# A convolution and an MLP in one kernel: three store pairs go to GpSimd's queue, and two transform visits move half a step

## The chip, the cores and the metric

The kernel runs on one core of a Trainium2 chip. A core has five engines, each with an instruction queue of its own that it works through in order: TensorE (PE, matmuls, with its weight loads shown apart as PEld), VectorE (DVE), ScalarE (ACT), GpSimd (POOL) and SyncE (SP), which here only issues transfers. Transfers are issued from the queues of SP, ACT and POOL; an issuing instruction that must wait holds up all that stands behind it in the same queue. The metric is the device time of one execution in microseconds (us); the median of 3 runs of the kernel before is 369.38 us (369.35 to 369.51).

## The reference

The inputs are q, k and v (2048 x 448 each), and weights. All is float32.

```python
xn = layernorm(q)
# A: an H3 layer
k_shift = sum_t k[s - 3 + t] * shift_k[:, 3 - t]        # 4 taps, causal
kv = k_shift * v
y  = causal_conv(kv, ssm_k) + kv * ssm_D                # length 2048 per channel, by FFT
A  = xn * y
# B: an MLP
B  = mish(xn @ w1 + b1) @ w2                            # 448 -> 1792 -> 448
out = q + A + B
```

## The kernel before

**Two jobs share the engines.** The MLP is the backbone. Its 2048 rows are cut into 8 chunks of 256, its 1792 hidden columns into 7 pairs of two 128-column blocks; chunk and pair together are numbered 0 to 55, and this text calls one such number a pair. Every float32 operand of the matmuls is split into a high part (`XH`, `w1h`, `w2h`, `ach`; cast on ACT) and a low part (`XL`, `w1l`, `w2l`, `acl`; the subtraction on DVE), and three products are summed. The long convolution runs as a two-stage Fourier transform in matmuls of their own, of which only the first stage matters here.

**The order is written out by hand.** The main loop (L637) runs over half steps `s`. Pair i has its first-layer matmuls, g1 (`g1_mm`, L457, 22 matmuls into a psum tile `pg`), in half step 2i. In half step 2i + 1 ACT applies mish (`mish`, L465) to it and splits the result into `ach` (L74) and `acl` (L75). Its second-layer matmuls, g2 (`g2_mm`, L482 to L484), follow two pairs later: half step 2i + 1 holds g2 of pair i - 2. All else is hung onto half steps: `at(slot, ...)` puts a call in front of a half step's own work, `after(slot, ...)` behind it. Within each engine the instructions stand exactly in the order in which the code issues them.

**The weights stream in during chunk 0.** Pieces of w1 and w2 are loaded by SP through four buffers `kr`, split (`w1_split`: ACT L340, DVE L345 and L347; `w2_split`: ACT and DVE in `split`, L74 and L75) and so free the buffer for a later load. g1 of pair 2 in half step 4 needs w1's third piece, whose split is hung in front of half step 4; g2 of pair 2 in half step 9 needs w2's third piece, split after half step 7.

**The first transform stage.** h (the convolution's kernel, `hT`) and kv come in 8 groups each. One group takes a *visit*: `f1_mm` (L125, 8 matmuls into two psum tiles `pc`; there are two such tiles in all), then `f1_fold` (ACT copies one half into a buffer `st`, L131; DVE forms sum and difference, L132 and L134), then `f1_out` (L140), which stores `st` to the scratch tensor `Dh` in DRAM in two transfers, one for each half of the partitions. There are two `st` buffers, so the copy L131 of a group waits until the stores of the group two visits earlier have landed. The head group, group 1, has its visit in half step 1 and its stores in half step 4. The other groups of h have theirs by the table `H_AT` (group: half step); the stores come three half steps after the visit. Group 2 comes next, then 3, then 0. The load of a group's input is issued five half steps ahead of its visit.

**POOL** normalises the rows of chunks 1 to 6 (`ln_parts`: L388, L392, L396), takes one of the four taps of kv per group (L155), and issues transfers only late in the program (`e_load` L284, and those of the last stage).

Of the kernel before, what the change touches and what calls it, by code (L numbers as in the profile page):

```python
# [22 lines left out]

G2_LAG = 2
H_HEAD = 1
H_AT = {2: 4, 3: 8, 0: 12, 4: 16, 5: 20, 6: 26, 7: 32}
KV_AT = (24, 29, 34, 39, 44, 50, 55, 60)
POOL_H = {20: (0, 2)}
H0_AT = 63
# [9 lines left out]
def tile_kernel(ctx: ExitStack, tc, q, k, v, sk, hT, sD, w1, b1, w2, c_f1, c_g, c_gi, c_i2, out):  # L39
    nc = tc.nc  # L40
# [15 lines left out]
    Dh = dp.tile([NO * 16, 32, D], F32, name="Dh")  # L56
# [32 lines left out]
    plan, plan2 = {}, {}  # L89

    def at(slot, fn, *args):
        plan.setdefault(int(slot), []).append((fn, args))

    def after(slot, fn, *args):
        plan2.setdefault(int(slot), []).append((fn, args))
# [38 lines left out]
        V.tensor_sub(st[:, 1], e, st[:, 1])  # L134
        dv()

    def f1_out(dst, g, key):
        st = ST.pop((key, g))
        for jj in range(2):
            nc.scalar.dma_start(dst.rearrange("(h p) n d -> p h n d", h=2)[:, :, 4 * g + 2 * jj:4 * g + 2 * jj + 2].rearrange("p h n d -> p h (n d)"),  # L140
                                st[64 * jj:64 * jj + 64].rearrange("p h b d -> p h (b d)"))

    def k_load(g):
# [385 lines left out]

    for g, t in H_AT.items():  # L530
        if g != 2:
            at(t - 5 if t > 7 else t - 3, h_load, g)
        if g == 0:
            after(t - 2, lambda: V.tensor_add(HT[0][0:1, 0], HT[0][0:1, 0], SD.pop()))
        at(t, f1_mm, HT, g, "h")
        if t in POOL_H:
            after(t, taps_pool, *POOL_H[t])
        after(t, f1_fold, g, "h")
        at(t + 3, f1_out, Dh, g, "h")

    at(12, lambda: nc.sync.dma_start(skb, sk.partition_broadcast(128)))
    for g in range(-2, 0):
# [1 line left out]
    for g, t in enumerate(KV_AT):  # L544
        d = t - (KV_AT[g - 1] if g else t - 6)
        at(t - d - (3 if g > 1 else 2), k_load, g)
        at(t - d - 1, v_load, g)
        for u in range(4):
            after(t - (2 if g else 1) - d + d * u / 4, taps, g, u)
        at(t, f1_mm, KV, g, "kv")  # L550
        if g + 1 < NO:
            after(t, taps_pool, g + 1, 2)
        after(t, f1_fold, g, "kv")
        at(t + 3, f1_out, Dkv, g, "kv")
# [9 lines left out]
    for o in range(NO):  # L564
        s, d = OCT_AT[0] + OCT_AT[1] * o, OCT_AT[1]
        h = s - 1 if o else H0_AT
# [66 lines left out]
    w1_lo(0, 128, 256)  # L633
    plan.setdefault(1, []).insert(0, (f1_mm, (HT, H_HEAD, "h")))
    plan2.setdefault(1, []).append((f1_fold, (H_HEAD, "h")))
    plan.setdefault(4, []).insert(0, (f1_out, (Dh, H_HEAD, "h")))
    for s in range(nslots):  # L637
        j = s // 2 - G2_LAG - 1
        if s % 2 == 0 and j >= 0 and pairs[j][1] == NP - 1:
# [75 lines left out]
```

## Time and profile before

| what | value |
|---|---|
| median of 3 runs | 369.38 us (369.35 to 369.51) |
| the profiled execution | 370.86 us |
| its span, first to last instruction | 368.9 us |
| granted TensorE clock over the span | 1.0 |
| PE busy | 98% |
| DVE, ACT, POOL busy | 71%, 45%, 19% |
| transfers, all queues | 79.35 MB, mean 215 GB/s |
| stores of h (`Dh<-st`), 16 of 448 KB, issued by ACT | 6.4 us to landing (median) |

A row of a timeline begins with the start in us from the span's beginning and the duration in us; then come engine, line, operation, output<-inputs, sizes, a count, and in brackets the idle time ahead of it with the work that ended it. Rows of groups end with the busy time in us, the mean of one in ns, and the idle time ahead. ACTq, SPq and POOLq are the parts of these engines that issue transfers. A wait row reads: who waited for whom, total us, times, longest.

### The profile page before, as it was taken

The numbers are of one execution on the slowest core, as the hardware profiler recorded it, in microseconds if no ns is written. First come the engines' busy times: TensorE is split into PE (matmuls) and PEld (weight loads), VectorE is DVE, ScalarE is ACT, GpSimd is POOL, SyncE is SP. The second block draws the span as 40 slices with busy tenths as digits, with TensorE's granted clock in tenths as the row PEclk, the third lists the DMA queues.
The fourth block names the chain that finished last, engine by engine and source line by source line (L and its number), as shares of the span: only waits on it lengthen the run. The fifth ranks groups of instructions, "written<-read, shape, count | busy, mean of one in ns | idle before, by whom it ended". The sixth has DMA issues, their size and how long they took to land.

```text
span 368.9 us, 7464 instructions
## 1 busy us (share of the span) xinstructions
PE 360.9 (98%) x3128; PEld 292.6 (79%) x3128; DVE 262.5 (71%) x359; ACT 166.3 (45%) x277; POOL 71.2 (19%) x58
## 2 busy tenths in 40 slices
PE   7998999999999999999999999999999999999995
PEld 2697888978888989889868666666666889889885
DVE  5897858999998888996515657656385752897751
ACT  3757543344241443253254555556655533235450
POOL 2005000920228222611006000060000005102020
PEclk9999999999999999999999999999999999999999
DMA  7998996839496329514675598896694375949655
GB/s 241 346 285 312 358 368 184 256 105 295 105 299 214 89 66 274 170 48 101 225 244 174 194 261 238 282 301 189 209 292 125 95 248 205 419 195 276 116 66 133
DMA packets 32354, 79.35 MB, mean 215 GB/s; under 512 B 2881, under 2 KB 19138, under 8 KB 32322
## 3 DMA queue, kind: packets, MB, share of 16 engines
q1 hardware_dynamic: 20210, 44.09, 35.8%
q10 hardware_dynamic: 9776, 22.88, 22.2%
q0 software_dynamic: 2336, 11.93, 11.3%
q8 instruction: 24, 0.39, 0.4%
q14 instruction: 8, 0.07, 0.1%
HBM read 50.44 MB, written 28.44 MB: 214 GB/s over the span
## 4 chain that ended last, share of the span: by engine, by line
PE 71%; DMA 12%; DVE 9%; POOL 3%; ACT 2%; issue 2%; SPq 0%; ACTq 0%; POOLq 0%; DVEq 0%
PE pg L457 27%; PE pg L482 10%; PE pg L484 9%; PE pg L483 9%; PE pc L208 7%; DMA kr<-in_w_dram 6%; PE pc L251 4%; PE pc L125 2%; PE pc L308 2%; DMA Dh<-st 2%; DVE x L172 2%; PE pg L407 2%; POOL xn L392 2%; DMA Dkv<-st 1%; DMA av<-Dkv 1%
## 5 line engine op out<-in xcount | busy, mean ns | idle before, releaser
L465 ACT ACTIVATE a<-pg,b1t 128x256 f32<-128x256 f32 x112 | 47.1, 472 | 113.0 <-PE pg L457 88.2
L457 PE MATMUL pg<-XH,w1h 128*128 128x256 f32 x448 | 91.3, 285 | 0.9 <-ACT XH L419 0.9
L75 DVE TENSOR_TENSOR acl<-a,ach 128x512 fp32r<-128x512 f32 x56 | 38.8, 693 | 65.0 <-ACT ach L74 64.7
L457 PEld LDWEIGHTS pg<-XH,w1h 128*128 128x128 f32 x448 | 69.6, 188 | 18.9 <-issue 15.7
L482 PE MATMUL pg<-w2h,ach 128*128 128x448 f32 x224 | 83.1, 371 | 0.0
L483 PE MATMUL pg<-w2l,ach 128*128 128x448 f32 x224 | 81.3, 363 | 0.9 <-DVE w2l L75 0.9
L484 PE MATMUL pg<-w2h,acl 128*128 128x448 f32 x224 | 81.4, 363 | 0.0
L457 PE MATMUL pg<-XL,w1h 128*128 128x256 f32 x448 | 69.6, 277 | 0.2 <-DVE XL L417 0.2
L457 PEld LDWEIGHTS pg<-XL,w1h 128*128 128x128 f32 x448 | 59.4, 188 | 0.4 <-DVE XL L417 0.4
L457 PE MATMUL pg<-XH,w1l 128*128 128x256 f32 x336 | 56.8, 277 | 0.0
L482 PEld LDWEIGHTS pg<-w2h,ach 128*128 128x128 f32 x224 | 42.0, 188 | 11.7 <-issue 9.4
L457 PEld LDWEIGHTS pg<-XH,w1l 128*128 128x128 f32 x336 | 46.8, 188 | 0.0
L483 PEld LDWEIGHTS pg<-w2l,ach 128*128 128x128 f32 x224 | 42.1, 188 | 3.6 <-DVE w2l L75 1.2
L484 PEld LDWEIGHTS pg<-w2h,acl 128*128 128x128 f32 x224 | 42.1, 188 | 2.5
L388 POOL TENSOR_TENSOR rstd<-ve,mhalf 128x2 f32<-128x2 f32 (+1 forms) x9 | 8.8, 977 | 156.2 <-DVE ve L385 156.1
L74 ACT CAST ach<-a 128x512 fp32r<-128x512 f32 x56 | 34.7, 620 | 1.8
L155 POOL TENSOR_TENSOR x<-kr,skb 128x896 f32<-128x896 f32 x8 | 17.1, 2133 | 83.6 <-DVE x L154 62.4
L392 POOL TENSOR_SCALAR xn<-qt,mv,rstd 128x448 f32<-128x448 f32 x12 | 27.8, 2320 | 0.6
L172 DVE TENSOR_TENSOR x<-x 128x896 f32<-128x896 f32 x24 | 26.8, 1115 | 1.4 <-POOL x L155 0.9
L131 ACT COPY st<-pc 128x896 f32<-128x896 f32 x16 | 14.5, 906 | 14.5 <-PE pc L125 12.6
L132 DVE TENSOR_TENSOR st<-pc,st 128x896 f32<-128x896 f32 x16 | 17.4, 1088 | 3.6 <-ACT st L131 3.1
L259 ACT COPY qe<-pc 128x896 f32<-128x896 f32 x16 | 13.8, 912 | 11.0 <-PE pc L251 10.8
(70 smaller groups left out, 389.7 us busy)
## 6 DMA issues: line engine op xcount, KB each, us to landing
Dh<-st ACTq DMA_DIRECT2D x16, 448.0 KB, 6.4
Dkv<-st ACTq DMA_DIRECT2D x16, 448.0 KB, 5.1
ah<-Dh SPq DMA_DIRECT2D x8, 896.0 KB, 7.0
av<-Dkv SPq DMA_DIRECT2D x8, 896.0 KB, 6.2
E<-qe ACTq DMA_DIRECT2D x16, 448.0 KB, 5.2
e<-E POOLq DMA_DIRECT2D x8, 896.0 KB, 7.9
kr<-in_k_dram SPq DMA_DIRECT2D x10, 448.0 KB, 6.7
x<-in_v_dram SPq DMA_DIRECT2D x8, 448.0 KB, 5.2
```

What stands on the lines that cost most here:

```text
L74: nc.scalar.copy(h, raw)
L75: V.tensor_sub(l, raw, h)
L132: V.tensor_add(st[:, 0], e, st[:, 1])
L155: nc.gpsimd.tensor_mul(o, KR[g - u // 2], skb[:, u:u + 1].to_broadcast([128, 2, D]))
L172: V.tensor_add(KV[g], KV[g], o)
L208: nc.tensor.matmul(p[32 * t:32 * t + 32, r, :D], g[rs, t, c], a[rs, t], start=True, stop=True, tile_position=(64 * r, 32 * t))
L392: eng.tensor_scalar(xn[:, jj, :D], Q[c][:, jj], mv[:, j, 0:1], rstd[:, j:j + 1], op0=ALU.subtract, op1=ALU.mult)
L457: nc.tensor.matmul(ps[:, n], l, r, start=n_ == 0, stop=n_ == len(mm) - 1)
L465: nc.scalar.activation(a[:, n], ps[:, n], AF.Mish, bias=b1t[:, 2 * p + n:2 * p + n + 1])
L482: nc.tensor.matmul(ps, ah[:, n, cs], w2h[:, f], start=f == 0, stop=False)
L483: nc.tensor.matmul(ps, ah[:, n, cs], w2l[:, f], start=False, stop=False)
L484: nc.tensor.matmul(ps, al[:, n, cs], w2h[:, f], start=False, stop=f == NF - 1)
```

## The change

`f1_out` gets the issuing engine as an argument. The head group's stores, and those of the groups whose visit stands before half step 12 (groups 2 and 3), are issued by GpSimd; those of the other five groups of h, and all of kv, stay with ScalarE. The visits of groups 2 and 3 move from half steps 4 and 8 to 5 and 9, and with them the fold, the stores (now in front of half steps 8 and 12) and group 3's load (from half step 3 to 4).

```diff
-H_AT = {2: 4, 3: 8, 0: 12, 4: 16, 5: 20, 6: 26, 7: 32}
+H_AT = {2: 5, 3: 9, 0: 12, 4: 16, 5: 20, 6: 26, 7: 32}
...
-    def f1_out(dst, g, key):
+    def f1_out(dst, g, key, eng=nc.scalar):
         st = ST.pop((key, g))
         for jj in range(2):
-            nc.scalar.dma_start(dst.rearrange("(h p) n d -> p h n d", h=2)[:, :, 4 * g + 2 * jj:4 * g + 2 * jj + 2].rearrange("p h n d -> p h (n d)"),
+            eng.dma_start(dst.rearrange("(h p) n d -> p h n d", h=2)[:, :, 4 * g + 2 * jj:4 * g + 2 * jj + 2].rearrange("p h n d -> p h (n d)"),
                                 st[64 * jj:64 * jj + 64].rearrange("p h b d -> p h (b d)"))
...
-        at(t + 3, f1_out, Dh, g, "h")
+        at(t + 3, f1_out, Dh, g, "h", nc.gpsimd if t < 12 else nc.scalar)
...
-    plan.setdefault(4, []).insert(0, (f1_out, (Dh, H_HEAD, "h")))
+    plan.setdefault(4, []).insert(0, (f1_out, (Dh, H_HEAD, "h", nc.gpsimd)))
```

The first place is PE at half step 4, with the waits of each instruction in brackets (the numbers name semaphores; `pg_216` is g1 of pair 1, `pg_269` before and `pg_259` after are g1 of pair 2). Before:

```order
L457 MATMUL pg_216<-XL,w1h 128x256 x4
L125 MATMUL pc<-x,f1id 64x448 [waits DMAHW1_49,Activation_49]
L125 MATMUL pc<-x,f1id 64x448
L125 MATMUL pc<-x,f1id 64x448 [waits DVE_49]
L125 MATMUL pc<-x,f1id 64x448 x5
L457 MATMUL pg_269<-XH,w1h 128x256 [waits Activation_49]
L457 MATMUL pg_269<-XH,w1h 128x256 x2
L457 MATMUL pg_269<-XH,w1l 128x256 [waits DVE_49]
```

After:

```order
L457 MATMUL pg_216<-XL,w1h 128x256 x4
L457 MATMUL pg_259<-XH,w1h 128x256 [waits Activation_49]
L457 MATMUL pg_259<-XH,w1h 128x256 x2
L457 MATMUL pg_259<-XH,w1l 128x256 [waits DVE_49]
L457 MATMUL pg_259<-XH,w1l 128x256 x2
L457 MATMUL pg_259<-XH,w1h 128x256 [waits DVE_49]
```

The visit of group 2 (L125) no longer stands between g1 of pair 1 and g1 of pair 2; it follows g1 of pair 2 and stands in front of g2 of pair 0.

The second place is ACT from group 2's copy to mish of pair 3 (`pg_338`). Before:

```order
L131 COPY st<-pc 128x896 [waits PE_49]
L465 ACTIVATE a<-pg_269,b1t 128x256 [waits PE_49]
L465 ACTIVATE a<-pg_269,b1t 128x256
L74 CAST ach<-a 128x512 [waits Activation_49]
L74 CAST w2h<-kr 128x896 [waits DMAHW6_49]
L340 CAST w1h<-kr 128x4x256 [waits DMAHW7_49]
L140 DMA Dh<-st 64x2x896 [waits DMAHW5_49,DVE_49]
L140 DMA Dh<-st 64x2x896 [waits DMAHW1_49]
L465 ACTIVATE a<-pg_338,b1t 128x256 [waits PE_49]
```

After:

```order
L465 ACTIVATE a<-pg_259,b1t 128x256 [waits DVE_49,PE_49]
L465 ACTIVATE a<-pg_259,b1t 128x256
L74 CAST ach<-a 128x512 [waits Activation_49]
L131 COPY st<-pc 128x896 [waits PE_49]
L74 CAST w2h<-kr 128x896 [waits DMAHW5_49]
L340 CAST w1h<-kr 128x4x256 [waits DMAHW6_49]
L465 ACTIVATE a<-pg_338,b1t 128x256 [waits DVE_49,PE_49]
```

The two stores with their waits are gone from in front of mish of pair 3, and the copy moves behind mish of pair 2. In DVE's order the fold moves behind `acl` of the same pair in the same way.

The third place is POOL around the normalisation of chunk 1 (`xn_328`), and the copy on ACT that uses a `st` buffer again. Before, on POOL:

```order
L388 TENSOR_TENSOR rstd_82<-ve_124,mhalf_79 128x1 x2
L388 TENSOR_TENSOR rstd_82<-ve_327,mhalf_79 128x2
L392 TENSOR_SCALAR xn_328<-qt_165,mv_81,rstd_82 128x448 x2
L396 COPY xn_328<-xn_328 128x2x64
L155 TENSOR_TENSOR x_795<-kr_531,skb_90 128x896
```

After (`st_209`, `st_317` and `st_449` are the head group, group 2 and group 3):

```order
L388 TENSOR_TENSOR rstd_82<-ve_124,mhalf_79 128x1 x2
L140 DMA Dh_75<-st_209 64x2x896 x2
L388 TENSOR_TENSOR rstd_82<-ve_327,mhalf_79 128x2
L392 TENSOR_SCALAR xn_328<-qt_165,mv_81,rstd_82 128x448 x2
L396 COPY xn_328<-xn_328 128x2x64
L140 DMA Dh_75<-st_317 64x2x896 x2
L140 DMA Dh_75<-st_449 64x2x896 x2
L155 TENSOR_TENSOR x_795<-kr_531,skb_90 128x896
```

And after, on ACT in half steps 12 to 13, where the copy is that of group 0:

```order
L419 CAST XH<-pg_535 128x4x128 [waits PE_49]
L131 COPY st<-pc 128x896 [waits DMASW3_49,DMASW2_49]
L465 ACTIVATE a<-pg_542,b1t 128x256 [waits DVE_49,PE_49]
L465 ACTIVATE a<-pg_542,b1t 128x256
L74 CAST ach<-a 128x512 [waits Activation_49]
L74 CAST w2h<-kr 128x896 [waits DMAHW7_49]
```

The stores of groups 2 and 3 now stand behind POOL's normalisation, and the copy of group 0 waits for two transfers of GpSimd's queue (DMASW), group 2's pair.

## The prediction

> **What bounds the kernel now.** I read the page first, then who TensorE (PE) waits for, then the chain of waits and the timelines of the stretch that the change touches.
>
> ```profile
> PE 360.9 (98%) x3128; PEld 292.6 (79%) x3128; DVE 262.5 (71%) x359; ACT 166.3 (45%) x277; POOL 71.2 (19%) x58
> ...
> PE pg L483 <- DVE w2l L75: 0.9, 1, 0.9
> ...
> PE pg L407 <- POOL xn L396: 0.3, 1, 0.3
> ...
> PE pc L208 <- DMA av<-Dkv: 0.3, 1, 0.3
> ```
>
> PE is the bound: only work taken off it, or a wait that ends on it, moves the end. After the prologue its only shown waits are 0.9, 0.3 and 0.3 us. But a matmul that started and then waits counts as busy, so I take PE's timeline from half step 4 to half step 10, and its weight loads:
>
> ```profile
> 15.70 1.98 PE L125 MATMUL pc<-x,f1id 32*64 32x448 f32 x16
> 17.61 0.62 PE L457 MATMUL pg<-XH,w1h 128*128 128x256 f32 x3
> ...
> 22.72 0.52 PE L457 MATMUL pg<-XH,w1h 128*128 128x256 f32 x3
> ...
> 27.81 1.01 PE L125 MATMUL pc<-x,f1id 32*64 32x448 f32 x16
> ...
> 31.45 0.47 PE L482 MATMUL pg<-w2h,ach 128*128 128x448 f32 x1
> ...
> 35.19 0.51 PE L457 MATMUL pg<-XH,w1h 128*128 128x256 f32 x3
> ...
> 16.68 0.22 PEld L125 LDWEIGHTS pc<-x,f1id 32*64 32x64 f32 x12 [0.79 <-DVE st L134]
> ```
>
> From 15.70 to 35.19 PE takes 19.49 us. For the same work without waits I use a later stretch, where g1 (one pair's first-layer matmuls), a visit (L125) and g2 (second-layer matmuls) follow each other in the order that the change makes:
>
> ```profile
> 86.78 0.52 PE L457 MATMUL pg<-XH,w1h 128*128 128x256 f32 x3
> ...
> 89.38 1.01 PE L125 MATMUL pc<-x,f1id 32*64 32x448 f32 x16
> 90.31 0.47 PE L482 MATMUL pg<-w2h,ach 128*128 128x448 f32 x1
> ...
> 92.83 0.52 PE L457 MATMUL pg<-XH,w1h 128*128 128x256 f32 x3
> ```
>
> So g1 is 2.60, a visit 0.93, g2 2.52, together 6.05 us; g1 and g2 without a visit are 27.81 - 22.72 = 5.09. The stretch holds three pairs and two visits: 2 x 6.05 + 5.09 = 17.19. It therefore waits 19.49 - 17.19 = 2.30 us, in two places: the visit at 15.70 lasts until 17.61, 0.98 too long (its psum buffers come free when DVE's fold L134 of the head group ends), and the remaining 1.32 us is the g2 block at 31.45. What is behind that block, from the chain of waits:
>
> ```profile
> 9.58 6.03 DMA kr<-in_w_dram
> ...
> 15.63 1.04 ACT w1h L340
> ...
> 17.45 0.62 ACT ach L74
> ...
> 20.06 8.35 DMA kr<-in_w_dram
> ...
> 28.44 0.58 ACTq L140
> ...
> 29.07 0.85 ACT a L465 x2
> ...
> 30.46 0.95 ACT w2h L74
> ...
> 31.43 1.39 DVE w2l L75
> ...
> 29.07 0.84 ACT L465 ACTIVATE a<-pg,b1t 128x256 f32<-128x256 f32 x2 [4.41 <-PE pc L125]
> ```
>
> The second store of group 2 sits in ScalarE's (ACT's) queue and is released at 28.44, the moment a load of w2 issued at 20.06 lands: the two share a DMA completion semaphore. Mish (L465) behind it starts at 29.07, after 4.41 us in which ACT stood idle; the cast of the same w2 piece starts at 30.46 though its data was there at 28.41; its low half on DVE ends at 32.82, and PE's L483 waits for it.
>
> **The change part by part.** *Stores taken from ACT.* Six issues leave ACT's queue. Without the store, w2h starts on landing at 28.41, ends at 29.4, and w2l ends at 30.5 to 30.8. PE now wants it at about 35.19 - 0.60 - 2.52 + 0.2 = 32.3 (0.60 is the gain worked out below). 1.5 us to spare: the 1.32 us wait goes, nothing is late next there.
>
> *The visit of group 2 behind g1 of pair 2.* The visit at 15.70 was in front of a g1 that could not have started then. That g1 needs w1's third piece, high half by ACT at 15.63 + 1.04 = 16.67, and low half by DVE:
>
> ```profile
> 15.54 1.09 DVE L134 TENSOR_TENSOR st<-pc,st 128x896 f32<-128x896 f32 x1
> 16.71 0.96 DVE L345 TENSOR_TENSOR w1l<-kr,w1h 128x768 fp32r<-128x768 f32 x1
> 17.70 0.42 DVE L347 TENSOR_TENSOR w1h<-kr,w1h 64x256 fp32r<-64x256 f32 x1
> ...
> 24.12 1.08 DVE L75 TENSOR_TENSOR w2l<-kr,w2h 128x896 fp32r<-128x896 f32 x1
> ```
>
> DVE's order up to there is unchanged, and L345 stands behind the fold that ends at 16.63, so an earlier landing gains at most 0.1 us. Unhindered from 15.70, the first three of 22 matmuls take 3 x 2.60/22 = 0.35 and the low-half ones would start at 16.05; they can start at 17.70, and the next one needs L347 at 18.12. Wait: 1.65 + 0.05 = 1.70 us, where the visit had hidden all but 0.98. The wait on the fold disappears inside it.
>
> *Sum.* Waits before 2.30, after 1.70: 0.60 us gained by half step 10. Span 368.9 becomes 368.3, the profiled run's 370.86 becomes 370.3; that run is 1.48 above the median of 369.38, which becomes 368.8. The single term is certain to about 0.15 either side (block lengths differ by 0.1).
>
> *The visit of group 3 behind g1 of pair 4.* At 27.81 it waits for nothing and takes the same 0.93 behind g1: nothing. Its load moves on SP behind a w1 load that waits for the buffer which L347 frees at 18.12, and has 12 us until the visit near 31, where the loads of that time land in 6 to 8.4 us (9.58 and 20.06 above): hidden. The loads in front of it come sooner.
>
> *DVE's fold behind acl.* The fold of group 2 waits for the visit's end, 15.70 + 1.70 + 2.60 + 0.93 = 20.9, and ACT's mish and cast (0.85 + 0.62 from 20.1), so ACT's copy runs 21.6 to 22.5, two folds of 1.09 to 24.7, w2l 1.09 to 25.8, against 24.12 + 1.08 = 25.2 before. PE wants it 2.52 + 2.60 + 0.2 after 20.9, at 26.2: hidden with 0.4 to spare. The two loads that SP issues after these buffers come free start 0.5 us later, with over 2 us in hand.
>
> *Stores in POOL's queue.* The head group's pair goes out while POOL idles. The pairs of groups 2 and 3 stand behind the normalisation of chunk 1, and this is new: nothing of the kind exists before.
>
> ```profile
> 30.59 0.69 DVE L75 TENSOR_TENSOR acl<-a,ach 128x512 fp32r<-128x512 f32 x1 [2.46 <-ACT ach L74]
> ...
> 29.02 4.00 POOL L392 TENSOR_SCALAR xn<-qt,mv,rstd 128x448 f32<-128x448 f32 x2
> 33.09 0.75 POOL L396 COPY xn<-xn 128x128 f32<-128x128 f32 x1
> ...
> 112.89 5.69 POOL L392 TENSOR_SCALAR xn<-qt,mv,rstd 128x448 f32<-128x448 f32 x2
> ...
> L284 POOL DMA_DIRECT2D e<-E x8: 714/732/984, 307.0 to 332.2; - x8
> ...
> L140 ACTq DMA_DIRECT2D Dh<-st x2: 582/1050/1517, 36.4 to 37.0; - x2
> ...
> DMA to landing us min/median/max: 9.0/9.8/10.5
> ...
> Dh<-st ACTq DMA_DIRECT2D x16, 448.0 KB, 6.4
> ```
>
> POOL ends the tail copy at 33.84, 0.5 later with DVE's fold: 34.3; the second store of group 2 is issued at 34.3 + 0.73 = 35.0. ACT's copy of group 0 (third use of that `st` buffer) waits for it, and mish of pair 6, and the cast of w2's sixth piece, are queued behind this copy. Landing time bounds: 6.4 (the median of all stores of h on the page) to 10.5 (the pair above, issued at the same time of the program on a busy DMA). I take 8.5, the middle: that pair had the same loads around it, which pulls up; but group 2's own 0.9 MB ran just ahead of it, and ahead of the pair in question there is no other store, which pulls down. Landing W = 43.5.
>
> ```profile
> 42.76 0.92 ACT L131 COPY st<-pc 128x896 f32<-128x896 f32 x1
> ...
> 47.15 1.09 DVE L75 TENSOR_TENSOR w2l<-kr,w2h 128x896 fp32r<-128x896 f32 x1
> ...
> 49.49 0.36 PE L482 MATMUL pg<-w2h,ach 128*128 128x448 f32 x1
> ...
> L75 DVE TENSOR_TENSOR acl<-a,ach 128x512 fp32r<-128x512 f32 x56 | 38.8, 693 | 65.0 <-ACT ach L74 64.7
> ```
>
> From W: copy 0.92, two folds 2.18, acl 0.69, w2l 1.09 = 4.9 us until w2l, which PE's L483 wants at 49.49 + 0.20 - 0.60 = 49.1. A landing up to W = 44.2 costs nothing, each us beyond costs one. With 43.5 it costs nothing; with 10.5 (W = 45.5) it costs 1.3, more than the gain. The Trainium skill, page "DMA: Bandwidth & Descriptors", section "Specifications", gives about 1 us to the first byte for a GpSimd issue and 0.6 for ScalarE; by that W would be 0.4 later, at 43.9, and the sum the same. No run here shows it yet.
>
> Behind half step 15 the order is the old one; the chains to PE's two waits of 0.3 start from PE itself and shift with it. So the gain stays.
>
> **The rivals.** *B, the late store eats the gain*: W between 44.2 and 45.5; time 368.8 to 370.1. For it: the 9.0 and 10.5 above. Against it: no store runs ahead of this pair.
>
> *C, slower*: one mechanism, POOL reaches the stores late. Its normalisation took 4.00 us at 29.02 but 5.69 at 112.89, while in the first case DVE had the 2.46 us hole before 30.59; after the change mish is not held up and that hole is mostly gone. With 1.7 us more the second store goes at 36.7; landed in 10.5, W = 47.2, a 3.0 us wait, net +2.4: 371.8. It decides from W = 45.5 on (370.1 and up). The Trainium skill, page "SBUF — State Buffer", section "Who interferes with whom", says a DVE instruction with two SBUF inputs and a GpSimd one that reads SBUF block each other in turn; by that rule the low-half subtractions (both inputs in SBUF) would stretch it. The trace agrees: 5.69 against 4.00.
>
> *D, the load of 20.06 was the real limit*: one 448 KB load is now directly in front of it. If it lands 1.5 us later than 28.41, PE waits again; wholly kept, the old 1.32 wait plus the 0.72 lost at 15.70 make 370.1. Against: the same bytes are queued ahead in both kernels, and the store issued at 23.67 is gone.
>
> *E, more gained*: the wait for w1's third piece doesn't appear. Up to 2.30: 367.1. Against it stands the fold that ends at 16.63.
>
> **How the numbers follow.** About 0.2% (0.74 us) is what a measurement of this kernel can tell from no change. The forecast (no store wait; own range 368.4 to 369.2) has 0.48, B 0.15, C 0.17, D 0.12, E 0.08. Faster (below 368.64): a third of the forecast's 0.48, E and a little of B, 0.26. Slower (above 370.12): C, most of D, 0.27. Within: 0.47. Range 368.0 to 370.9: it leaves out E and C's upper half.
>
> **What would show it.** Right: PE's visit at about 20 us without a wait, g1 of pair 2 waiting about 1.7 us for w1l at 16 to 18; no ACT gap at 24 to 29; L483 at 32 without a wait; PE 0.6 us earlier at half step 10. POOL's second store near 35.0 and landed before 44.2. Wrong: ACT's copy L131 held past 44.2 by a store and L483 waiting near 49; or w2l ending after 32.3.

## The result, and the profile after

The changed kernel takes 371.69 us (median of 10 runs, 370.25 to 372.50), the kernel before beside it 369.49 us (10 runs): a ratio of 1.0053, 95% interval 1.0039 to 1.0068. It is slower by 2.0 us (1.4 to 2.5), where 0.6 us faster was predicted; 371.69 lies above the upper end of the range, 370.9. The time profiled is 371.69 us, its span 369.9 us.

TensorE (PE) in the changed kernel, from its timeline: the visit of the head group, g1 of pair 2 with its wait, the visit of group 2 and g2 of pair 0, g1 of pair 5 (half step 10), the g2 block of half step 15 with its wait and the visit behind it, and the visit of group 5 (half step 20), behind which the two kernels run alike (from there to the end 305.8 us after, 305.95 before).

```profile
12.48 1.01 PE L125 MATMUL pc<-x,f1id 32*64 32x448 f32 x16
...
16.24 0.62 PE L457 MATMUL pg<-XH,w1h 128*128 128x256 f32 x3
...
18.05 0.62 PE L457 MATMUL pg<-XH,w1l 128*128 128x256 f32 x3 [1.19 <-DVE w1l L345]
...
20.59 1.01 PE L125 MATMUL pc<-x,f1id 32*64 32x448 f32 x16
21.52 0.47 PE L482 MATMUL pg<-w2h,ach 128*128 128x448 f32 x1
...
35.11 0.52 PE L457 MATMUL pg<-XH,w1h 128*128 128x256 f32 x3
...
49.50 0.36 PE L482 MATMUL pg<-w2h,ach 128*128 128x448 f32 x1
...
50.72 0.47 PE L483 MATMUL pg<-w2l,ach 128*128 128x448 f32 x1 [0.85 <-DVE w2l L75]
...
53.12 1.01 PE L125 MATMUL pc<-x,f1id 32*64 32x448 f32 x16
...
64.09 1.01 PE L125 MATMUL pc<-x,f1id 32*64 32x448 f32 x16
```

The reader is to see two waits. g1 of pair 2 starts at 16.24 and waits for `w1l`: the stretch to half step 10 lasts 35.11 - 16.24 = 18.87 us, the predicted 17.19 + 1.70 = 18.89 almost to the digit. And the g2 block of half step 15 lasts 53.12 - 49.50 = 3.62 us, where the same block before lasted 51.99 - 49.49 = 2.50: 1.12 us that the forecast did not have.

The chain of work that leads to the second wait (start, duration, what):

```profile
31.39 4.71 POOL xn L392 x2
...
36.16 0.29 POOL xn L396
36.44 0.64 POOL Dh L140
37.08 8.74 DMA Dh<-st
...
45.90 0.92 ACT st L131
...
49.58 1.09 DVE w2l L75
...
50.72 0.47 PE pg L483
```

And the copy on ScalarE (ACT), from its timeline:

```profile
45.90 0.91 ACT L131 COPY st<-pc 128x896 f32<-128x896 f32 x1 [3.04 <-DMA Dh<-st]
```

This is rival C's mechanism: GpSimd (POOL) reaches the stores behind its normalisation, group 2's second store lands at 37.08 + 8.74 = 45.82, and the copy of group 0, with mish and w2's cast queued behind it, hangs on it.

### The profile page after: what moved, and what is told of

Its sections match the earlier page's. It is cut to its first block, busy times and chain, and to the rows that moved or that the text cites. A ratio compares the mean times of both kernels' runs of the same rounds, so it can differ in the third digit from the quotient of the medians.

```text
span 369.9 us, 7473 instructions
## 1 busy us (share of the span) xinstructions
PE 360.6 (97%) x3128; PEld 292.9 (79%) x3128; DVE 262.3 (71%) x359; ACT 166.5 (45%) x277; POOL 75.1 (20%) x64
## 4 chain that ended last, share of the span: by engine, by line
PE 71%; DVE 8%; issue 7%; POOL 6%; DMA 5%; ACT 2%; SPq 0%; POOLq 0%; DVEq 0%; ACTq 0%
PE pg L457 27%; PE pg L482 10%; PE pg L484 9%; PE pg L483 9%; PE pc L208 7%; PE pc L251 4%; POOL xn L392 3%; DMA Dh<-st 2%; PE pc L308 2%; POOL x L155 2%; DMA kr<-in_w_dram 2%; DVE x L172 2%; PE pc L125 2%; DVE st L132 1%; PE pg L407 1%
```

## The experiments

Eleven runs were made, of nine kernels (`_again` marks a kernel that was run a second time), in three groups, each on a chip of its own; each group shares its runs of the kernel before (medians 369.43, 369.31 and 369.60 us). A ratio is that of a run to its group's kernel before. Two theories were put against each other first. S: the late store alone makes the loss, and the wait of 1.32 us near 32 us belongs to every execution of the kernel before. V: the visit moved behind g1 makes it, and the 1.32 us wait was an accident of the one execution profiled. What came out of the first group, that both losses are real and separate, was then tested as "two losses".

**The kernel before once more (b_again)**, unchanged.

> The kernel before, unchanged, for a second trace of it. Its first trace came from a run 1.5 us slower than its median. Theory V (the time is lost at half step 4, and the 1.32 us wait of g2 near 32 us is not there in an ordinary run of the kernel before) expects a span near 367.6 with that wait below 0.5 us. Theory S (the late store of group 2 alone makes the loss) expects the wait near 1.3 us again and the span within 0.5 us of 368.9. Ratio 1.000 by both.

Measured: 369.12 us, ratio 0.9986 (0.9970 to 1.0002); profiled at 369.55 us with a span of 367.6, where the first profiled execution had 370.86 and 368.9. PE and ACT in this second execution of the same program:

```profile
12.39 1.01 PE L125 MATMUL pc<-x,f1id 32*64 32x448 f32 x16
...
16.12 1.98 PE L125 MATMUL pc<-x,f1id 32*64 32x448 f32 x16
...
18.03 0.62 PE L457 MATMUL pg<-XH,w1h 128*128 128x256 f32 x3
...
34.12 0.51 PE L457 MATMUL pg<-XH,w1h 128*128 128x256 f32 x3
...
61.88 1.01 PE L125 MATMUL pc<-x,f1id 32*64 32x448 f32 x16
```

```profile
24.69 1.60 ACTq L140 DMA_DIRECT2D Dh<-st  x2
26.34 0.84 ACT L465 ACTIVATE a<-pg,b1t 128x256 f32<-128x256 f32 x2 [0.66 <-PE pg L457]
```

The pair of stores, which held ACT for 5.35 us in the first execution (its row follows), holds it for 1.60 us here; mish starts at 26.34, and no wait for `w2l` is in the timeline of PE. From the visit at 16.12 to half step 10 it takes 18.00 us, 1.49 less than in the first execution. The visit itself is as long as there (16.12 to 18.03, 1.91 us, so 0.98 too long again). The difference is the g2 block of pair 2, 2.41 us against 3.74, and 0.15 us in g1 of pairs 3 and 4 (2.52 and 2.62 us against 2.59 and 2.70). The first execution:

```profile
23.67 5.35 ACTq L140 DMA_DIRECT2D Dh<-st  x2
```

V is right on this point: this second execution, 0.4 us above its median, doesn't have the 1.32 us.

**The stores without the visits (e1_stores_only)**, the changed kernel but for

```diff
-H_AT = {2: 5, 3: 9, 0: 12, 4: 16, 5: 20, 6: 26, 7: 32}
+H_AT = {2: 4, 3: 8, 0: 12, 4: 16, 5: 20, 6: 26, 7: 32}
```

> The stores of the first three groups go to GpSimd, the visits stay at half steps 4 and 8. S: the second store of group 2 still goes out behind the normalisation, near 35 to 36 us, and lands near 45; ACT's copy of group 0 waits for it, w2l of pair 5 ends near 50 and PE waits there for 1 to 2 us: 0.5 to 1.5 us slower than before. V: the visits hide the w1 wait again and ACT's stall is gone, so it is not slower than before, between 0 and -1.3 us.

Measured: 370.36 us, ratio 1.0019 (1.0002 to 1.0035). Its chain of work:

```profile
30.31 4.71 POOL xn L392 x2
...
35.08 1.19 POOL xn L396
36.27 0.64 POOL Dh L140
36.92 7.85 DMA Dh<-st
...
44.85 0.92 ACT st L131
```

The copy waits as in the changed kernel, and the block of half step 15 is 52.07 - 48.05 = 4.02 us long, 1.52 too long. The late store is a loss by itself, without any visit moved: 0.7 us by the ratio (0.1 to 1.3). The profiled execution shows more than that, so the size of this wait differs from execution to execution. V allowed no loss here, so V alone falls.

**The visits without the stores (e2_visits_only)**: the kernel before with the table of the changed one.

```diff
-H_AT = {2: 4, 3: 8, 0: 12, 4: 16, 5: 20, 6: 26, 7: 32}
+H_AT = {2: 5, 3: 9, 0: 12, 4: 16, 5: 20, 6: 26, 7: 32}
```

> The visits move to half steps 5 and 9, ScalarE keeps all stores. S: without the late store of group 2 nothing holds the copy of group 0; within 0.7 us of before. V: the whole loss stays, about +1.7 to 2 us.

Measured: 370.42 us, ratio 1.0019 (1.0003 to 1.0034). g1 of pair 2 waits 1.42 us for `w1l` at 19.83; the copy of group 0 starts at 44.54 without a wait, and the block of half step 15 is 2.49 us long. In the times this loss is as large as e1's (0.7 us, 0.1 to 1.3), not the 1.7 us or more that V needed; S allowed up to 0.7 us here, but not this wait for `w1l`. S and V each explain a part.

**The store of group 2 ahead of the normalisation (e4_early_store)**: the changed kernel with group 2's pair issued in half step 6.

```diff
-        at(t + 3, f1_out, Dh, g, "h", nc.gpsimd if t < 12 else nc.scalar)
+        at(t + (1 if g == 2 else 3), f1_out, Dh, g, "h", nc.gpsimd if t < 12 else nc.scalar)
```

> The changed kernel, with group 2's stores issued two half steps earlier, so that they stand ahead of the normalisation in GpSimd's queue. They go out when the fold ends, near 25.3 us, and land by 35. S: the copy of group 0 waits for nothing, the wait of PE near 50 us is gone, about 1.1 us (its size in the trace: 53.12 - 51.99) less than the changed kernel or more. V: the same time as the changed kernel, +2 us over before.

Measured: 370.33 us, ratio 1.0021 (1.0006 to 1.0035). POOL issues the pair at 25.85, ahead of the normalisation; the copy starts at 43.08 without a wait, and the block of half step 15 is 52.31 - 49.81 = 2.50 us. The second loss is gone, the first one stays.

**Neither loss (e5_unmoved_early, e5_again)**: visits as before, all six stores on POOL, group 2's pair in half step 6. Against the changed kernel:

```diff
-H_AT = {2: 5, 3: 9, 0: 12, 4: 16, 5: 20, 6: 26, 7: 32}
+H_AT = {2: 4, 3: 8, 0: 12, 4: 16, 5: 20, 6: 26, 7: 32}
...
-        at(t + 3, f1_out, Dh, g, "h", nc.gpsimd if t < 12 else nc.scalar)
+        at(t + (2 if g == 2 else 3), f1_out, Dh, g, "h", nc.gpsimd if t < 12 else nc.scalar)
```

> Stores of the first three groups on GpSimd, visits at half steps 4 and 8 as before, and group 2's stores issued in half step 6, ahead of the normalisation. Now the theory is two separate losses: a late store of group 2 (about 1.2 us between the second trace of before and the changed kernel) and the visit that no longer covers w1's wait (0.9 us). It expects neither loss here: within 0.3 us of before, with no wait of PE near 50 us. The rival, that a store on GpSimd costs by itself (descriptors, other order of the transfers), expects +0.5 us or more.

> Visits unmoved, all three store pairs on GpSimd, group 2's pair in half step 6, once more with five rounds: whether this form is faster than the kernel before. Two losses: no wait of either kind, a ratio of 0.998 to 1.000. A gain that counts would be below 0.998; the rival that GpSimd's stores cost something by themselves gives 1.001 or more.

Measured: 368.96 us, ratio 0.9984 (0.9962 to 1.0006), and again 368.98 us, ratio 0.9988 (0.9967 to 1.0009). POOL of the first of them:

```profile
17.28 1.46 POOL L140 DMA_DIRECT2D Dh<-st  x2 [10.71 <-DVE st L134]
23.88 1.20 POOL L140 DMA_DIRECT2D Dh<-st  x2 [5.14 <-DVE st L134]
...
30.39 4.70 POOL L392 TENSOR_SCALAR xn<-qt,mv,rstd 128x448 f32<-128x448 f32 x2
35.16 1.19 POOL L396 COPY xn<-xn 128x128 f32<-128x128 f32 x1
36.30 1.29 POOL L140 DMA_DIRECT2D Dh<-st  x2
```

Neither loss is there. Stores issued by POOL show no cost of their own (the intervals leave at most 0.2 and 0.3 us); what counts is behind which work in its queue they stand. Both ratios lie below 1, but both intervals reach beyond it: that this form beats the kernel before isn't shown.

**One visit at a time (e6_visit2, e7_visit3, e7_again)**: the kernel before with group 2's entry alone at 5, or group 3's alone at 9.

```diff
-H_AT = {2: 4, 3: 8, 0: 12, 4: 16, 5: 20, 6: 26, 7: 32}
+H_AT = {2: 5, 3: 8, 0: 12, 4: 16, 5: 20, 6: 26, 7: 32}
```

> Before, with group 2's visit alone moved to half step 5. Two losses: g1 of pair 2 waits 1.7 us for w1l where the visit had left 0.8 to 0.98: +0.7 to +0.9 us. Rival (the move of group 3 and of its load costs): 0.

Measured: 370.31 us, ratio 1.0037 (1.0016 to 1.0057), that is 1.4 us (0.6 to 2.1). g1 of pair 2 waits for `w1l`:

```profile
19.38 0.63 PE L457 MATMUL pg<-XH,w1l 128*128 128x256 f32 x3 [1.07 <-DVE w1l L345]
```

The whole loss of e2 is in this visit.

```diff
-H_AT = {2: 4, 3: 8, 0: 12, 4: 16, 5: 20, 6: 26, 7: 32}
+H_AT = {2: 4, 3: 9, 0: 12, 4: 16, 5: 20, 6: 26, 7: 32}
```

> Before, with group 3's visit alone moved to half step 9 and its load to half step 4. Two losses: 0 within 0.3 us. Rival: +0.7 us.

> Only group 3's visit moved, once more, since the first interval took in both zero and 0.3%. If this move costs nothing, a ratio of 0.999 to 1.001 and no wait of PE between half steps 8 and 15; if it costs, 1.0015 or more, and a wait of PE in half steps 9 to 11 that the kernel before lacks.

Measured: 369.73 us, ratio 1.0016 (0.9998 to 1.0034), and again 370.22 us, ratio 1.0010 (0.9990 to 1.0030). Both intervals hold zero and a small loss, so whether group 3's move costs a few tenths isn't settled by the times. In the traces it is 0.1 us (last column of the table of executions below). The second execution had a wait that the first lacks, in half step 7, ahead of the visit of group 3. ACT, then PE:

```profile
18.25 1.68 ACTq L140 DMA_DIRECT2D Dh<-st  x1
19.97 1.05 ACT L340 CAST w1h<-kr 128x1024 fp32r<-128x1024 f32 x1 [0.92 <-issue]
...
24.74 3.70 ACTq L140 DMA_DIRECT2D Dh<-st  x2
```

```profile
26.36 0.48 PE L483 MATMUL pg<-w2l,ach 128*128 128x448 f32 x1 [0.55 <-DVE w2l L75]
```

The wait of PE at 26.36 goes back to the head group's second store, the first of these rows: it took 1.68 us of ACT's queue, where it took 0.62 in b_again, so the cast behind it started at 19.97, and with it DVE's splits, the fold and the `w2l` that PE wants came later. The g2 block lasts 28.68 - 25.46 = 3.22 us for it. Group 2's pair, the last row, held ACT for 3.70 us, but mish of pair 3 behind it was in time: g2 of pair 2 lasts 34.73 - 32.21 = 2.52 us. So a stall of ACT by these stores was no single event, but the wait of PE behind it was: in six profiled executions with group 2's stores on ACT the two stood there as one block of 5.35, 1.60, 2.86 and 3.70 us (before, b_again, e7, e7_again) or went out in 0.6 us each (e2, e6), and only behind the 5.35 us did g2 of pair 2 wait.

**Group 3's pair first (e8_late_store)**: the changed kernel with the order of the two pairs in POOL's queue exchanged.

```diff
-        at(t + 3, f1_out, Dh, g, "h", nc.gpsimd if t < 12 else nc.scalar)
+        at(t + {2: 7, 3: 2}.get(g, 3), f1_out, Dh, g, "h", nc.gpsimd if t < 12 else nc.scalar)
```

> The changed kernel with GpSimd's two late pairs in the other order: group 3's first, group 2's behind. Group 2's second store then goes out about 1.3 us later and lands near 47. Each us of landing behind 44.2 costs one us, so the wait of PE near 50 us grows from 1.2 to about 2.5 us: +1.3 us over the changed kernel, +3.3 over before. Rival (the order in that queue doesn't matter, GpSimd's stores cost by themselves): the changed kernel's time, +2.

Measured: 370.55 us, ratio 1.0045 (1.0022 to 1.0067): 1.7 us over the kernel before by the ratio, 1.2 by the medians (two of its 12 runs, 372.34 and 373.99 us, stand far above the rest). The larger loss that two losses were to give did not come. The time is near the rival's, but e5 speaks against its ground, a cost of GpSimd's stores by themselves. The premise was wrong, as the order of the instructions shows: on POOL, group 3's buffer `st_447` now goes out ahead of group 2's `st_317`, and ACT's copy of group 0 waits for the third and fourth transfer of that queue, as it did in the changed kernel.

```
L140 DMA Dh_75<-st_447 64x2x896 [waits DVE_49]
L140 DMA Dh_75<-st_447 64x2x896
L140 DMA Dh_75<-st_317 64x2x896 x2
```

```
L131 COPY st_565<-pc_519 128x896 [waits DMASW3_49,DMASW2_49,DVE_49]
```

The copy takes the buffer that is released first, whichever group it held. So the experiment didn't delay the store at all. POOL's timeline, and the copy from ACT's:

```profile
30.02 3.91 POOL L392 TENSOR_SCALAR xn<-qt,mv,rstd 128x448 f32<-128x448 f32 x2
34.00 0.29 POOL L396 COPY xn<-xn 128x128 f32<-128x128 f32 x1
36.17 2.46 POOL L140 DMA_DIRECT2D Dh<-st  x4 [1.89 <-DVE st L134]
...
44.45 0.91 ACT L131 COPY st<-pc 128x896 f32<-128x896 f32 x1 [2.02 <-DMA Dh<-st]
```

The copy started at 44.45, earlier than in the changed kernel (45.90), and PE lost only 0.11 us in half step 15 of this execution. With the 0.9 us of the visit that is 1.0 us, near the 1.2 of the medians; whether the two long runs had the store later stays open. It is a point of the table on the store below.

**The changed kernel once more (after_again)**, unchanged.

> The changed kernel once more, unchanged. If both losses are its ordinary course: a ratio of 1.004 to 1.007 to the kernel before; in the trace g1 of pair 2 waits 1.2 to 1.7 us for w1l in half step 4, the copy of group 0 waits for a store of h until 44.2 us or later, and the g2 block in half step 15 is longer than 2.50 us by as much as this copy starts less than 4.7 us ahead of that block. Rival, that the late store was an accident of one execution: no wait in half step 15, and a ratio of 1.002 to 1.003.

Measured: 371.24 us, ratio 1.0043 (1.0016 to 1.0070), span 369.0. The two waits on PE, and the chain to the second:

```profile
15.99 0.62 PE L457 MATMUL pg<-XH,w1h 128*128 128x256 f32 x3 [0.69 <-ACT w1h L340]
...
17.08 0.62 PE L457 MATMUL pg<-XH,w1l 128*128 128x256 f32 x3 [0.47 <-DVE w1l L345]
...
49.88 0.47 PE L483 MATMUL pg<-w2l,ach 128*128 128x448 f32 x1 [1.03 <-DVE w2l L75]
```

```profile
29.91 4.79 POOL xn L392 x2
...
35.05 0.64 POOL Dh L140
35.69 9.29 DMA Dh<-st
...
45.06 0.92 ACT st L131
```

The wait in g1 of pair 2 is 0.69 us for `w1h` and 0.47 for `w1l` here, 1.16 together and a little below the expected 1.2; the copy starts at 45.06, 3.42 us ahead of its g2 block, and the block is 3.80 us long, 1.30 too long (4.7 - 3.42 = 1.28 expected). The interval of the times alone wouldn't exclude the rival's 1.002 to 1.003; both profiled executions of the changed kernel have both losses.

**All executions side by side.** The start of the program differs between executions of one kernel: the head group's visit began anywhere between 11.50 and 14.26 us in these thirteen, so spans can't be compared directly. Below, the first column counts from the head visit's start to g1 of pair 5 (half step 10), the second from there to the visit of group 5 (half step 20).

| execution | visit of group 2 | group 2's stores | to half step 10 | half steps 10 to 20 |
|---|---|---|---|---|
| before (370.86 us) | in front of g1 | ACT, held 5.35 us | 23.21 | 27.76 |
| b_again | in front | ACT | 21.73 | 27.76 |
| e5 / e5_again | in front | POOL, half step 6 | 21.79 / 21.62 | 27.77 / 27.77 |
| e7 / e7_again | in front | ACT, held 2.86 / 3.70 us | 21.72 / 22.54 | 27.85 / 27.86 |
| e1 | in front | POOL, behind normalisation | 21.80 | 29.52 |
| e6 | behind | ACT | 22.61 | 27.76 |
| e2 | behind | ACT | 22.62 | 27.86 |
| e4 | behind | POOL, half step 6 | 23.26 | 27.86 |
| e8 | behind | POOL, behind normalisation | 22.59 | 27.96 |
| after / after_again | behind | POOL, behind normalisation | 22.63 / 22.59 | 28.98 / 29.16 |

The first column depends on the place of group 2's visit: 21.6 to 21.8 us with it in front, 22.6 behind, 0.9 us more, except where a store on ACT made PE wait (before and e7_again) or, in e4, w1's third piece came later still (a wait of 1.51 us for `w1h` at 17.42). The second depends on the stores behind the normalisation (in e1 1.52 us of it is in the block of half step 15, 0.2 stands just ahead of that block). Where group 3's visit moves, 0.1 is added. For the changed kernel this makes 0.9 + 1.2 = 2.1 us against b_again, where the spans differ by 369.9 - 367.6 = 2.3.

**How late a store may land.** The prediction let the store land until 44.2 with the block of half step 15 at 49.49 - 0.60 = 48.89, that is 4.69 us ahead of this block, and charged one us for each us beyond. (e8's landing is its copy's start less 0.08, the gap in the changed kernel.)

| execution | landing | g2 block of half step 15 | ahead | wait by the prediction | block over 2.50 us |
|---|---|---|---|---|---|
| e8 | 44.37 | 49.06 | 4.69 | 0.00 | 0.11 |
| after | 45.82 | 49.50 | 3.68 | 1.01 | 1.12 |
| after_again | 44.98 | 48.48 | 3.50 | 1.19 | 1.30 |
| e1 | 44.77 | 48.05 | 3.28 | 1.41 | 1.52 |

Four points on a line of slope one, 0.11 us above the prediction's.

## Why the prediction was wrong

*"The 1.32 us wait goes": wrong, and the first step that failed.* It went, but it was not there to be gained in an ordinary execution. The profiled execution before ran 1.48 us above the median, and its first column is 23.21 - 21.73 = 1.48 us longer than b_again's. That is the 1.32 us wait (3.74 - 2.41 = 1.33 for this g2 block) and 0.15 us in g1 of pairs 3 and 4; the visit waits equally long in both. The prediction had this excess before its eyes, took it off to come to the median, and took the 1.32 us, which made up most of it, off once more as a gain. Without that, the first term is a loss: 1.70 - 0.98 = 0.72 us by the prediction's own figures, 18.87 - 18.00 = 0.87 by the runs. That ACT's stores cost nothing on average isn't shown either: in e7_again another of them, the head group's, cost 0.8 us; and e5, which takes the stores off ACT and loses nothing elsewhere, is at 0.9984 and 0.9988, which would be 0.4 to 0.6 us, and neither interval excludes zero.

*"Wait: 1.65 + 0.05 = 1.70 us" in g1 of pair 2: right.* 18.87 - 17.19 = 1.68 measured. The reasoning that the visit had covered most of this wait was right too; e6 shows its loss alone.

*"Landing W = 43.5. With 43.5 it costs nothing": wrong, the second step that failed.* The limit and the slope were right (table above); W was 1.8 us too early, counted from the head visit: 45.82 - 12.48 = 33.34 against 43.5 - 11.98 = 31.52. Of that the landing time is a small part (8.74 against 8.5). The issue is 24.60 against 23.02 us behind the head visit: POOL's normalisation begins 1.37 later than assumed, takes 4.70 instead of 4.00 us, and the tail copy is 0.46 shorter. It begins later because VectorE's (DVE's) statistics do, behind a piece of w1 that lands later. In the changed kernel, ACT and then DVE and POOL:

```profile
26.00 1.05 ACT L340 CAST w1h<-kr 128x1024 fp32r<-128x1024 f32 x1 [2.17 <-DMA kr<-in_w_dram]
```

```profile
27.08 0.96 DVE L345 TENSOR_TENSOR w1l<-kr,w1h 128x768 fp32r<-128x768 f32 x1 [0.84 <-ACT w1h L340]
...
29.93 0.17 DVE L385 TENSOR_SCALAR ve<-mv 128x2 f32<-128x2 f32 x1
```

```profile
30.18 1.10 POOL L388 TENSOR_TENSOR rstd<-ve,mhalf 128x2 f32<-128x2 f32 x1 [11.27 <-DVE ve L385]
```

Why this piece of w1 landed later stays open. The 4.00 us too came from that one execution before: there DVE stood idle for 2.46 us, until 30.59, because mish was held up. In ten of the thirteen executions, b_again among them, the normalisation takes 4.70 to 4.79 us. The others are this one, e7 with 4.29 and e8 with 3.91. By the rule of the Trainium skill, page "SBUF — State Buffer", section "Who interferes with whom", DVE instructions with two SBUF inputs and GpSimd ones that read SBUF block each other. These runs agree with it only in part: DVE was idle for 0.67 us within the short normalisation of e8, but for 0.40 us within that of after_again too, which is the longest, 4.79 us. That an idle DVE made the 4.00 us is argued, not shown.

*Rival C: its side came true, and POOL's lateness, but not its sizes.* It named the late POOL and 371.8 us (measured 371.69), but reached this by a 3.0 us wait less the 0.6 gained. Measured were a wait of 1.1 and a loss of 0.9 where the forecast counted the gain; and the normalisation was 0.7 us longer where C had 1.7, but began 1.37 later. That the two numbers agree is luck. Rival B had the store's cost of up to 1.3 right. Rival D, a late load, left no wait on `w2l` near 32; E did not happen.

*What the two steps make.* The first is off by 0.60 + 0.87 = 1.47 us, the second by 1.12; with 0.1 for group 3's visit that is 2.7 of the 2.9 us between the 368.8 forecast and the 371.69 measured.

*The smaller steps.* Group 3's visit: 0.1 us in the trace, not more than 0.3% in the times. DVE's fold behind `acl`: no wait of PE followed in half steps 5 to 9. Behind half step 20: alike, as forecast. By the Trainium skill, page "DMA: Bandwidth & Descriptors", section "Specifications", with its longer first byte for a GpSimd issue, W would have been 0.4 later, an estimate; no run separates this, since landings alone went from 7.85 to 9.29 us.

## What to carry to other kernels

Before a wait of one profiled execution is counted as a gain, hold that execution's time against the median. An excess of the same size as the wait is a warning, not a proof (e2's profiled execution ran 1.9 us above its median without such a wait, with a head visit that began at 14.26); a second profile of the same kernel decides it, as b_again did here. A store moved to a less busy engine inherits that engine's queue: here it was not the number of busy us on POOL that decided, but a pair of instructions of 4.7 us in front of the store, and the same store ahead of that pair showed no loss. And independent work that stands in front of a block that has to wait is cover; moved behind it, it gives the wait back.

## What the runs showed of the hardware that was not expected

The same program with the same order on every queue differs from execution to execution, the kernel before by 1.48 us up to half step 10 (23.21 and 21.73). ACT's pair of stores held it for 5.35 us in one execution of the kernel before and for 1.60 in the other, and the head visit of e7's kernel began at 13.83 in one execution and at 12.19 in the other. GpSimd's normalisation of the same two tiles took 3.91 to 4.79 us over all executions. And the six GpSimd stores of the changed kernel landed 4.2 to 11.3 us after their issue (median 9.0), with the same 448 KB each.
